# Convolution and feed-forward on one core: an inverse transform's buffer, two norms and two sums moved

## The chip, the cores and the metric

The kernel runs on one core of a Trainium2 chip. Its engines work side by side, each through its own list of instructions, and meet at semaphores: PE (TensorE, matrix products into PSUM), ACT (ScalarE), DVE (VectorE), POOL (GpSimd) and SP (SyncE, which here only issues transfers). PEld is PE's loading of weights. The metric is the device time of one execution in microseconds, lower is better. Before the change the median of three runs is 269.0 us (267.62 to 269.3).

## The reference

S = 2048 rows of D = 640 numbers, a feed-forward width of 1728, all in bfloat16. With `LN` a layer norm without weights, the core of it is:

```
k_shift[s] = sum over t < 4 of k[s - t] * shift_k[:, t]       # a causal convolution of 4 taps
kv         = k_shift * v
y          = causal convolution of kv with ssm_k over all 2048 rows (FFT) + kv * ssm_D
h          = q + LN(q) * y
out        = h + (silu(LN(h) @ w_gate) * (LN(h) @ w_up)) @ w_down
```

## The kernel before, in words

The 2048 rows are taken in four blocks of 512, named 0 to 3. The long convolution is done by blocks: every block of kv and every block of ssm_k is transformed by matrix products with cosine and sine tables (a transform of 256 odd frequencies, two planes for the real and the imaginary part), the products of block j of kv with block i - j of ssm_k are summed for output block i, and one inverse transform by matrix products gives y of block i.

For a block i the steps, with the names used in this document and their lines, are:

- `kv` (line 697): k's block is loaded transposed into the tile `kT` by a transposing transfer (line 514, issued by SP), v's block into `vt`. PE does the four taps as three groups of products with diagonal matrices (L717 and L712, "convolutions"), ACT evicts them to `kT` (L502), and for blocks 1 to 3 five transposing transfers turn them into `kvo`; DVE multiplies into `vt` (L748).
- `xfwd` (line 750): PE transforms `vt` in eight tasks of four products ("halves", L610) or, for block 2, eight tasks of two ("quarters", L647). ACT evicts each (L502); DVE combines them (L581, L656).
- `prod` (line 768): per pair of blocks and per half `f2`, DVE multiplies a transformed block by a kernel block twice (L779, L780, 2560 numbers a partition), adds and subtracts (L785, 1280 numbers), and for j > 0 adds the result to `Y` (L796, 2560 numbers). Last come the butterflies into `IE` and `IO` (L581), the inverse's input: sums and differences.
- `inverse` (line 847): PE makes four tiles of 128 rows (tasks 0 to 3; L860). Tasks 1 and 3 read `IO`, 0 and 2 read `IE`. Then, per tile, h and its layer norm (the "second norm"). In blocks 1 to 3 ACT evicts y to SBUF with a bias (L884), DVE multiplies it into `xh` (L887), ACT sums the row (L898) and sums its squares (L900). In block 0 (`ST`) one DVE instruction reads PSUM, multiplies and sums (L874), POOL makes the mean (L878), and ACT sums squares (L880). In both forms ACT adds epsilon (L904), POOL takes the power -1/2 (L911), and ACT (blocks 1 to 3: mean times scale L914, then L916) or DVE (block 0, L919) writes the normed row to `qo`. SP transposes it into `hnT` (L514).
- `ffn` (line 926, called ff0 to ff3): 14 "gate tasks" of PE (L941 and L942, ten products each; L952 for the narrow last), ACT's silu and copy (L964, L966), DVE's product (L968), then the "down tasks" (L1003) with two small pair tasks (L1015). In blocks 0 to 2 ACT evicts the result (L1023) and DVE adds it (L1030); SP writes the block out.

PSUM has four tiles of two banks (`units=4`), handed out by the planner in order of release. A task of PE that opens a tile waits for all who read the tile's earlier content.

What sets the order. Every instruction group is a numbered task with a cost estimate. `ORDER` is a written list of task numbers for each of the five engines; each engine issues strictly in it. `schedule` walks the lists with the estimated costs only to hand out PSUM tiles, to choose pauses and to place fill products; `emit` writes the waits. So an instruction of SP that waits (a transfer whose target is still being read) holds every later transfer of SP, and the same is true for POOL. Fill products (L250, 192 columns) are matmuls without use, which the planner puts where it expects PE to idle.

Memory is laid out by hand (lines 410 to 467). `kT` and `IO` share bytes, and so do `hnT` and `IE`. Because of that the load of block i + 1 of k cannot begin before the inverse of block i has read `IO`. `vt` has its bytes for itself. `VECTOR` lists the PSUM evictions that DVE does in place of ACT.

Of the kernel before, what the change touches and what calls it, by code (L numbers as in the profile page):

```python
# [11 lines left out]
ACTF = mybir.ActivationFunctionType  # L12
# [46 lines left out]
class _Graph:  # L59
# [87 lines left out]
    def schedule(self, order):  # L147
# [4 lines left out]
        for t in self.tasks:  # L152
            for d in t.deps | t.after:
                d.succ.append(t)
        seq = {e: [self.tasks[int(x)] for x in order[e].split()] for e in ENGINES}
        assert sorted(t.seq for e in ENGINES for t in seq[e]) == list(range(len(self.tasks)))
# [12 lines left out]
        while len(self.glob) < len(self.tasks):  # L169
# [22 lines left out]
            if t.opens is not None:  # L192
                pt = t.opens
                u = min((u for u in range(self.units) if unit_by[u] is None), key=lambda u: unit_free[u])
                pt.unit = u
                left[pt] = len(pt.users)
                t.late = t.deps - set(last_users.get(u, ()))
                t.deps.update(last_users.get(u, ()))
                if self.warm is not None and e == "pe" and at[e] > 2:
                    idle = s - max(free[e], unit_free[u])  # L200
                    t.fill = int((idle - 250) / 83) if idle > 700 else 0
                unit_by[u] = pt
# [28 lines left out]
    def emit(self, block):  # L231
# [77 lines left out]
    "pe": """  # L309
# [7 lines left out]
    """,  # L317
    "act": """
# [12 lines left out]
    """,  # L331
    "dve": """
# [10 lines left out]
    """,  # L343
    "pool": """
        8 10 6 11 5 9 7 151 202 216 195 205 209 219 198 212 134 336 135 403 421 394 412 529 610 619 628 601 736 822 813 840
        831
    """,
    "sp": """
# [3 lines left out]
    """,  # L352
}

VECTOR = """
    21 129
"""

def bass_sequential_preLN__ssm_conv_h3__swiglu_ffn__prompt_kernel(
# [38 lines left out]
    with ExitStack() as es:  # L398
# [23 lines left out]
        kT = sb("kT", o + 5120, [NC5, N + 16])  # L422
        IO = sb("IO", o + 5120, [2, 2, D])
        hnT = sb("hnT", o + 10400, [NC5, N])
# [43 lines left out]

        BN, DIRECT, D8, PT, BN2, ST, R4, PAIR, WARM, ACC, EA, KD, RD, LA, RA = (0,), (), (), (0,), (), (0,), ('xf2',), True, 24, (), True, (2, 3), (), (1, 2, 3), (0, 1, 2)
        g = _Graph(nc, es)  # L470
# [4 lines left out]
        def cact(n, ptr=0):  # L475
            return 60 + 0.833 * n + 93 * ptr

# [327 lines left out]
        def ln1(i):  # L805
# [18 lines left out]
            if EA:  # L824
                g.add("act", nm, lambda e: e.activation(out=s[:, 2, :], in_=s[:, 1, :], func=ACTF.Identity, bias=epc[:, 0:1]), 160,  # L825
                      r=[s[:, 1, :], epc[:, 0:1]], w=[s[:, 2, :]])
            else:
                g.add("pool", nm, lambda e: e.tensor_scalar(out=s[:, 2, :], in0=s[:, 1, :], scalar1=LN_EPS * D, scalar2=None, op0=ALU.add), 260,
                      r=[s[:, 1, :]], w=[s[:, 2, :]])
# [17 lines left out]
        def inverse(i):  # L847
# [18 lines left out]
            for j in range(4):  # L866
# [35 lines left out]
                if EA:  # L902
                    ep = epc[:, int(st):int(st) + 1]
                    g.add("act", nm, lambda e, m=m, ep=ep: e.activation(out=m[:, 2:3], in_=m[:, 1:2], func=ACTF.Identity, bias=ep), 160,  # L904
                          r=[m[:, 1:2], ep], w=[m[:, 2:3]])
# [7 lines left out]
                if i in LA:  # L913
                    g.add("act", nm, lambda e, m=m: e.activation(out=m[:, 4:5], in_=m[:, 0:1], func=ACTF.Identity, scale=m[:, 3:4]), 160,  # L914
                          r=[m[:, 0:1], m[:, 3:4]], w=[m[:, 4:5]])
# [10 lines left out]
        def ffn(i):  # L926
# [3 lines left out]
            for fb in range(14):  # L930
# [30 lines left out]
                for rows, ps_g, ps_u, ts in parts:  # L961
                    n = ts.stop - ts.start
                    uv, gv = u[rows, ts], gt[rows, 0:n]
                    g.add("act", nm, lambda e, pt=pt, gv=gv, a=ps_g, ts=ts: e.activation(out=gv, in_=pt.f(a[0], N, a[1])[:, ts], func=ACTF.Silu, scale=gain),  # L964
                          cact(n), w=[gv], pr=[pt])
                    g.add("act", nm, lambda e, pt=pt, uv=uv, a=ps_u, ts=ts: e.activation(out=uv, in_=pt.f(a[0], N, a[1])[:, ts], func=ACTF.Copy, scale=gain),  # L966
                          cact(n), w=[uv], pr=[pt])
                    g.add("dve", nm, lambda e, uv=uv, gv=gv: e.tensor_tensor(out=gv, in0=gv, in1=uv, op=ALU.mult),  # L968
                          cdve(n), r=[gv, uv], w=[gv])
            dn, pair = {}, ()  # L970
# [145 lines left out]
```

## Time and profile before

| what | us |
|---|---|
| median of three runs | 269.0 |
| the profiled execution | 268.22 |
| its span, first to last instruction | 266.3 |
| PE, DVE, ACT, POOL busy | 254.0, 204.0, 203.9, 29.1 |
| first gate task of ff0, ff1, ff2, ff3 begins | 52.5, 112.2, 170.0, 219.2 |
| last product of PE ends | 263.6 |

The profile is of one execution. A row of a group gives line, engine, operation, tiles, form and count, then the busy time in us, the mean of one in ns, and the idle time of the engine just ahead of it with what ended most of it. The chain of waits goes back from the last instruction to whatever released each step. A matmul's end is modelled, so consecutive matmuls overlap in the rows, and the same is true of ACT and DVE by about 0.1 us.

### The profile page before, as it was taken

The page shows a single profiled execution, that of the slowest core. Times are in us where ns is not written, and L with a number is a line of the kernel's source. Part 1 is how long each engine was busy: PE and PEld are TensorE (multiplying, and loading weights), DVE is VectorE, ACT ScalarE, POOL GpSimd, SP SyncE. Part 2 cuts the span into 40 slices and gives each one's busy share as a digit, 9 for nine tenths or more (in the row PEclk, how much of TensorE's full clock was granted, in tenths as well). Part 3 has the DMA queues.
Part 4 walks back from the last instruction along what each step waited for, and adds up shares of the span by engine and source line. Part 5 has one row for each costly group of instructions (what it writes and reads, how often), then busy time and mean ns, then how long its engine had stood idle before and what let it go on. Part 6 is the DMA issues. An engine that isn't in the chain of part 4 may idle for free.

```text
span 266.3 us, 4177 instructions
## 1 busy us (share of the span) xinstructions
PE 254.0 (95%) x1638; PEld 142.1 (53%) x1638; DVE 204.0 (77%) x285; ACT 203.9 (77%) x392; POOL 29.1 (11%) x37
## 2 busy tenths in 40 slices
PE   7889888999999999999999999899999999999995
PEld 5567454545544646544445567444446674444563
DVE  0889999999999999999999999999895101330404
ACT  2689999999967999766979999678799982653600
POOL 0000314202030035000020041000300200000000
PEclk9999999999999999999999999999999999999999
DMA  6998919889966566331001734510000140000032
GB/s 155 335 333 266 342 57 227 131 194 315 178 111 108 81 173 105 55 117 81 4 0 19 184 79 93 146 78 1 2 0 0 22 79 0 0 2 0 0 127 74
DMA packets 43701, 28.47 MB, mean 107 GB/s; under 512 B 32289, under 2 KB 41378, under 8 KB 43682
## 3 DMA queue, kind: packets, MB, share of 16 engines
q1 hardware_dynamic: 41968, 25.58, 36.4%
q0 software_dynamic: 1056, 2.62, 5.7%
q8 instruction: 13, 0.21, 0.3%
q10 hardware_dynamic: 658, 0.01, 0.1%
q14 instruction: 6, 0.05, 0.1%
HBM read 15.69 MB, written 2.62 MB: 69 GB/s over the span
## 4 chain that ended last, share of the span: by engine, by line
PE 53%; ACT 23%; DVE 11%; DMA 6%; SPq 4%; issue 2%; POOL 0%; DVEq 0%
PE ps L941 16%; PE ps L942 15%; PE ps L1003 14%; SPq L514 3%; ACT xh L843 3%; ACT KT L502 3%; PE ps L610 2%; DMA kT<-in_A_k_dram 2%; ACT KO L502 2%; DMA ftab<-cst_ftab 2%; DMA hnT<-qo 2%; DVE gu L968 2%; PE ps L717 2%; ACT C L502 1%; ACT qo L884 1%
## 5 line engine op out<-in xcount | busy, mean ns | idle before, releaser
L1003 PE MATMUL ps<-Wd,gu 128*128 128x384 bf16 (+1 forms) x390 | 55.5, 299 | 0.1
L941 PE MATMUL ps<-hnT,GA 128*128 128x512 bf16 x140 | 53.1, 379 | 1.3 <-DMA hnT<-qo 1.1
L942 PE MATMUL ps<-hnT,UA 128*128 128x512 bf16 x140 | 53.1, 379 | 0.0
L1003 PEld LDWEIGHTS ps<-Wd,gu 128*128 128x128 bf16 x390 | 37.6, 98 | 17.1 <-issue 1.1
L941 PE MATMUL ps<-hnT,GB 128*128 128x512 bf16 x120 | 45.5, 379 | 0.0
L942 PE MATMUL ps<-hnT,UB 128*128 128x512 bf16 x120 | 45.5, 379 | 0.0
L966 ACT ACTIVATE ub<-ps 128x512 bf16<-128x512 f32 (+1 forms) x60 | 33.9, 567 | 14.9 <-PE ps L942 12.0
L964 ACT ACTIVATE gu<-ps 128x512 bf16<-128x512 f32 x52 | 30.4, 596 | 13.2 <-PE ps L942 13.1
L968 DVE TENSOR_TENSOR gu<-gu,ub 128x512 bf16<-128x512 bf16 x52 | 21.5, 421 | 23.8 <-ACT gu L964 15.8
L779 DVE TENSOR_TENSOR T<-X,C 128x2560 bf16<-128x2560 bf16 x20 | 29.7, 1486 | 0.2
L780 DVE TENSOR_TENSOR T<-X,C 128x2560 bf16<-128x2560 bf16 x20 | 29.7, 1486 | 0.1
L911 POOL TENSOR_TENSOR mv<-mv,half 128x1 f32<-128x1 f32 x16 | 16.1, 1010 | 69.1 <-ACT mv L904 69.1
L941 PEld LDWEIGHTS ps<-hnT,GA 128*128 128x128 bf16 x140 | 13.7, 98 | 18.4 <-DMA hnT<-qo 1.4
L610 PE MATMUL ps<-KT,ftab 128*128 128x320 bf16 x128 | 19.8, 300 | 3.5 <-ACT KT L502 1.1
L942 PEld LDWEIGHTS ps<-hnT,UA 128*128 128x128 bf16 x140 | 13.7, 98 | 15.6
L785 DVE TENSOR_TENSOR T<-T 128x1280 bf16<-128x1280 bf16 x24 | 19.5, 820 | 0.2
L941 PEld LDWEIGHTS ps<-hnT,GB 128*128 128x128 bf16 x120 | 11.7, 98 | 14.2 <-ACT gu L964 0.2
L942 PEld LDWEIGHTS ps<-hnT,UB 128*128 128x128 bf16 x120 | 11.8, 98 | 14.0
L831 POOL TENSOR_TENSOR st<-st,half 128x8 f32<-128x8 f32 x4 | 8.3, 2067 | 88.1 <-ACT st L825 88.1
L796 DVE TENSOR_TENSOR Y<-Y,T 128x2560 bf16<-128x2560 bf16 x12 | 17.8, 1484 | 0.0
L610 PEld LDWEIGHTS ps<-KT,ftab 128*128 128x128 bf16 x128 | 11.2, 98 | 10.9 <-ACT KT L502 2.0
L843 ACT ACTIVATE xh<-xh,st 128x640 bf16<-128x640 bf16 x16 | 14.7, 967 | 2.7 <-DVE st L833 2.7
(96 smaller groups left out, 381.9 us busy)
## 6 DMA issues: line engine op xcount, KB each, us to landing
kc<-in_A_ssm_k_dram SPq DMA_DIRECT2D x4, 640.0 KB, 9.4
xh<-in_A_q_dram SPq DMA_DIRECT2D x4, 640.0 KB, 4.1
vt<-in_A_v_dram SPq DMA_DIRECT2D x4, 640.0 KB, 4.5
out_dram<-xh SPq DMA_DIRECT2D x15, 160.0 KB, 1.9
Wd<-in_B_w_down_dram SPq DMA_DIRECT2D x1, 1280.0 KB, 6.3
C<-C POOLq DMA_DIRECT2D x1, 1280.0 KB, 9.6
C<-R POOLq DMA_DIRECT2D x1, 1280.0 KB, 9.4
UA<-in_B_w_up_dram SPq DMA_DIRECT2D x1, 1120.0 KB, 9.1
```

Source lines behind the costliest of these rows:

```text
L610: last = e.matmul(pt.f(c, W), ftab[:, cs, j, f * P:(f + 1) * P], src[:, j, c * W:(c + 1) * W], start=(j == par), stop=(j == par + 2))
L779: g.add("dve", nm, lambda e, x=x, k=k, t1=t1: e.tensor_tensor(out=t1, in0=x, in1=k, op=ALU.mult), cdve(2560), r=[x, k], w=[t1])
L780: g.add("dve", nm, lambda e, x=x, k=ksw, t2=t2: e.tensor_tensor(out=t2, in0=x, in1=k, op=ALU.mult), cdve(2560), r=[x, k], w=[t2])
L785: g.add("dve", nm, lambda e, p=p, q=q, d=d, op=op: e.tensor_tensor(out=d, in0=p, in1=q, op=op), cdve(1280), r=[p, q], w=[d])
L796: g.add("dve", nm, lambda e, y=y, z=z: e.tensor_tensor(out=y, in0=y, in1=z, op=ALU.add), cdve(2560), r=[y, z], w=[y])
L843: g.add("act", nm, lambda e, j=j, xj=xj: e.activation(out=xj, in_=xj, func=ACTF.Identity, scale=s[:, 4, j:j + 1], bias=s[:, 5, j:j + 1]), ...
L941: e.matmul(pt.f(0, N), wg[:, c, f0:f0 + P], hnT[:, c, :], start=(c == 0), stop=(c == NC5 - 1))
L942: last = e.matmul(pt.f(1, N), wu[:, c, f0:f0 + P], hnT[:, c, :], start=(c == 0), stop=(c == NC5 - 1))
L964: g.add("act", nm, lambda e, pt=pt, gv=gv, a=ps_g, ts=ts: e.activation(out=gv, in_=pt.f(a[0], N, a[1])[:, ts], func=ACTF.Silu, scale=gain) ...
L966: g.add("act", nm, lambda e, pt=pt, uv=uv, a=ps_u, ts=ts: e.activation(out=uv, in_=pt.f(a[0], N, a[1])[:, ts], func=ACTF.Copy, scale=gain) ...
L968: g.add("dve", nm, lambda e, uv=uv, gv=gv: e.tensor_tensor(out=gv, in0=gv, in1=uv, op=ALU.mult), cdve(n), r=[gv, uv], w=[gv])
L1003: last = e.matmul(pt.flat(c1 - c0, P + c0), slots[fb][:, j * P:(j + 1) * P], Wd[:, fb, c0:c1], start=(fb == 0 and not second), stop=(fb == ...
```

## The change

Three edits of the computation, and a new order for all engines.

1. `IO` moves from the bytes of `kT` to those of `vt` (one line). k's next block now waits only for the transposes of this block's convolutions; v's next block waits for the inverse.
2. `ST` grows from block 0 to blocks 0, 1 and 2: the second norms of blocks 1 and 2 take the form with the DVE instruction from PSUM (L874, L878, L880) in place of the eviction, the product and the sum (L884, L887, L898). The apply stays on ACT. Block 2's first norm gets one small negation on DVE.
3. `ACC` grows from none to the pairs (1, 3) and (2, 3): their results go to the tile `ZB` (in the place of the kernel's block 3 transform) and are added to `Y` by four transfers that POOL issues with an adding operation, 640 KB each, in place of four DVE additions (L796).

With these the orders of all engines are replaced, the evictions that DVE takes (`VECTOR`) are two others, the fill products are named by task (`FILL`: six ahead of block 0's first convolution, eight ahead of block 1's) in place of being placed by the planner (eight and six in the trace), and some of the planner's cost estimates change.

What moves in the new order, of what the prediction speaks of: SP issues k's block 1 directly after GA and ahead of kc3, itab and UA; k's block 2 behind block 1's transposes and half of the weights; k's block 3 after the first of the four transposes of block 1's second norm. PE does the convolutions of block 2 within ff0's gate tasks and around the inverse of block 1, and those of block 3 within the start and the gate tasks of ff1, ahead of the inverse of block 2. The inverse of block 2 stands after the first down task of ff1. On ACT the mean-times-scale of a row of blocks 1 and 2 stands directly or nearly so after the epsilon of the same row.

```
-        IO = sb("IO", o + 5120, [2, 2, D])
+        IO = sb("IO", o, [2, 2, D])
...
-        ..., (0,), ('xf2',), True, 24, (), True, (2, 3), (), (1, 2, 3), (0, 1, 2)
+        ..., (0, 1, 2), ('xf2',), True, 24, ((1, 3), (2, 3)), True, (2, 3), (), (1, 2, 3), (0, 1, 2)
...
+        fills = dict(tuple(map(int, x.split(":"))) for x in FILL.split())
...
-                if self.warm is not None and e == "pe" and at[e] > 2:
-                    idle = s - max(free[e], unit_free[u])
-                    t.fill = int((idle - 250) / 83) if idle > 700 else 0
+                if self.warm is not None and e == "pe":
+                    t.fill = fills.get(t.seq, 0)
...
+FILL = "20:6 313:8"
...
 VECTOR = """
-    21 129
+    83 85
 """
```

`VECTOR` before: block 0's first convolution (1024 columns) and one half of kernel block 3. After: two halves of kernel block 1. The lists of `ORDER` are too long to print; the text above says what of them matters.

More of the change, by code (lines that the diff above doesn't have):

```diff
@@ L309 @@
     "pe": """
[7 rows of a table removed]
[7 rows of a table added]
     """,
     "act": """
[12 rows of a table removed]
[11 rows of a table added]
     """,
     "dve": """
[10 rows of a table removed]
[10 rows of a table added]
     """,
     "pool": """
-        8 10 6 11 5 9 7 151 202 216 195 205 209 219 198 212 134 336 135 403 421 394 412 529 610 619 628 601 736 822 813 840
-        831
+        10 5 6 8 9 11 7 151 202 216 209 205 219 195 212 198 134 336 135 414 417 398 406 409 390 401 393 525 618 621 610 602
+        594 613 605 597 767 772 777 782 729 815 806 833 824
     """,
     "sp": """
[3 rows of a table removed]
[3 rows of a table added]
     """,
 }
+FILL = "20:6 313:8"
 VECTOR = """
-    21 129
+    83 85
 """
@@ L467, in bass_sequential_preLN__ssm_conv_h3__swiglu_ffn__prompt_kernel @@
         assert o + 576 <= SBB + 16481 - A0, o + 576
-        BN, DIRECT, D8, PT, BN2, ST, R4, PAIR, WARM, ACC, EA, KD, RD, LA, RA = (0,), (), (), (0,), (), (0,), ('xf2',), True, 24, (), True, (2, 3), (), (1, 2, 3), (0, 1, 2)
+        BN, DIRECT, D8, PT, BN2, ST, R4, PAIR, WARM, ACC, EA, KD, RD, LA, RA = (0,), (), (), (0,), (), (0, 1, 2), ('xf2',), True, 24, ((1, 3), (2, 3)), True, (2, 3), (), (1, 2, 3), (0, 1, 2)
         g = _Graph(nc, es)
@@ L475, in cact @@
         def cact(n, ptr=0):
-            return 60 + 0.833 * n + 93 * ptr
+            return 60 + 0.833 * n + (93 * ptr if ptr < 2 else 219)
         def cdve(n):
@@ L824, in ln1 @@
             if EA:
-                g.add("act", nm, lambda e: e.activation(out=s[:, 2, :], in_=s[:, 1, :], func=ACTF.Identity, bias=epc[:, 0:1]), 160,
+                g.add("act", nm, lambda e: e.activation(out=s[:, 2, :], in_=s[:, 1, :], func=ACTF.Identity, bias=epc[:, 0:1]), 185,
                       r=[s[:, 1, :], epc[:, 0:1]], w=[s[:, 2, :]])
@@ L903, in inverse @@
                     ep = epc[:, int(st):int(st) + 1]
-                    g.add("act", nm, lambda e, m=m, ep=ep: e.activation(out=m[:, 2:3], in_=m[:, 1:2], func=ACTF.Identity, bias=ep), 160,
+                    g.add("act", nm, lambda e, m=m, ep=ep: e.activation(out=m[:, 2:3], in_=m[:, 1:2], func=ACTF.Identity, bias=ep), 185,
                           r=[m[:, 1:2], ep], w=[m[:, 2:3]])
@@ L913, in inverse @@
                 if i in LA:
-                    g.add("act", nm, lambda e, m=m: e.activation(out=m[:, 4:5], in_=m[:, 0:1], func=ACTF.Identity, scale=m[:, 3:4]), 160,
+                    g.add("act", nm, lambda e, m=m: e.activation(out=m[:, 4:5], in_=m[:, 0:1], func=ACTF.Identity, scale=m[:, 3:4]), 185,
                           r=[m[:, 0:1], m[:, 3:4]], w=[m[:, 4:5]])
@@ L964, in ffn @@
                     g.add("act", nm, lambda e, pt=pt, gv=gv, a=ps_g, ts=ts: e.activation(out=gv, in_=pt.f(a[0], N, a[1])[:, ts], func=ACTF.Silu, scale=gain),
-                          cact(n), w=[gv], pr=[pt])
+                          max(400, cact(n)), w=[gv], pr=[pt])
                     g.add("act", nm, lambda e, pt=pt, uv=uv, a=ps_u, ts=ts: e.activation(out=uv, in_=pt.f(a[0], N, a[1])[:, ts], func=ACTF.Copy, scale=gain),
-                          cact(n), w=[uv], pr=[pt])
+                          max(400, cact(n)), w=[uv], pr=[pt])
                     g.add("dve", nm, lambda e, uv=uv, gv=gv: e.tensor_tensor(out=gv, in0=gv, in1=uv, op=ALU.mult),
-                          cdve(n), r=[gv, uv], w=[gv])
+                          max(320, cdve(n)), r=[gv, uv], w=[gv])
             dn, pair = {}, ()
```

63 rows, old and new, of the table ORDER are left out of this document.

## The prediction

> **What bounds the kernel now.** I read the page's busy shares first, then busy time by stretch, then the chain of waits and the timeline at the places where PE stands still, and the groups by form for prices.
>
> ```profile
> PE 254.0 (95%) x1638; PEld 142.1 (53%) x1638; DVE 204.0 (77%) x285; ACT 203.9 (77%) x392; POOL 29.1 (11%) x37
> ```
>
> The columns of the next view are the stretch, its length, and the busy time of PE, PEld, DVE, ACT and POOL, then clock and DMA share.
>
> ```profile
> 0.00:17.30 17.30, 14.16 (x130) 9.81 (x131) 8.61 (x15) 8.60 (x11) 0.63 (x11) 1.00 0.92 261
> 17.30:52.50 35.20, 31.52 (x274) 20.39 (x273) 34.48 (x51) 34.99 (x58) 6.95 (x9) 1.00 0.77 214
> 52.50:88.00 35.50, 35.50 (x182) 17.38 (x181) 35.09 (x49) 30.18 (x58) 4.57 (x3) 1.00 0.78 178
> 88.00:112.00 24.00, 23.02 (x181) 14.00 (x178) 23.75 (x29) 22.23 (x47) 5.92 (x4) 1.00 0.61 115
> 112.00:142.00 30.00, 29.83 (x141) 13.70 (x142) 29.52 (x41) 23.19 (x50) 1.89 (x1) 1.00 0.14 45
> 142.00:171.00 29.00, 27.80 (x218) 17.76 (x216) 28.78 (x36) 28.18 (x55) 4.36 (x4) 1.00 0.49 115
> 171.00:266.30 95.30, 92.22 (x523) 49.09 (x521) 43.75 (x69) 56.49 (x117) 4.81 (x5) 1.00 0.11 28
> ```
>
> There are two regimes. From 17.3 to 52.5 ACT is busy 34.99 of 35.20 us (it empties PSUM) and PE only 31.52: this stage ends when ACT does. From 52.5 on PE is the bound: idle 0.00, then 0.98 (88 to 112), 0.17, 1.20 (142 to 171), and 3.08 in the last stretch, most of it the tail after the last product. DVE looks full up to 171 (35.09 of 35.50), but it fills its time with products of later blocks, and PE does not wait for it. So the matmul work, which the change leaves as it is, sets the end; only PE's waits can be won. The waits at the two block boundaries:
>
> ```profile
> 88.69 2.35 PE L860 MATMUL ps<-IE,itab 128*128 128x320 bf16 x16
> 94.37 1.06 PE L717 MATMUL ps<-kT,dg 64*64 64x512 bf16 x16 [0.61 <-DMA kT<-in_A_k_dram]
> 148.12 1.25 PE L860 MATMUL ps<-IE,itab 128*128 128x320 bf16 x8
> 170.05 0.39 PE L941 MATMUL ps<-hnT,GA 128*128 128x512 bf16 x1 [1.09 <-DMA hnT<-qo]
> ```
> ```profile
> 88.61 3.61 SPq L514 DMA_TRANSPOSE kT<-in_A_k_dram  x1
> 103.01 6.39 SPq L514 DMA_TRANSPOSE hnT<-qo  x4
> ```
> ```profile
> SPq L514 <- PE ps L860: 55.2, 2, 28.2
> ```
> ```profile
> PE ps L860 <- ACT qo L884: 0.4, 1, 0.4
> ```
> ```profile
> 25.19 2.26 ACT KT L502 x2
> 29.34 0.60 ACT KO L502
> 47.81 2.17 PE ps L610 x16
> 98.69 7.06 PE ps L1003 x52
> 105.75 0.38 PE ps L1015 x4
> 110.87 1.25 ACT FO L502 x2
> 112.17 0.39 PE ps L941
> 149.31 0.72 ACT qo L898 x2
> 150.03 0.68 ACT qo L884
> 153.24 0.91 ACT kT L502
> 165.69 4.31 DMA hnT<-qo
> ```
>
> The load of k's next block stands in SP's queue until the inverse has read IO (55.2 us in two waits), starts at 88.61, and costs PE 0.61 at 94.37. At 112.17 PE waits for evictions (ACT FO), at 170.05 for the transposed second norm (1.09), and in the last stretch 0.4 at the inverse of block 3 (L860).
>
> **The change part by part.** Prices by form:
>
> ```profile
> L796 DVE TENSOR_TENSOR Y<-Y,T 128x2560 bf16<-128x2560 bf16 x12 | 17.8, 1484 | 0.0
> L779 DVE TENSOR_TENSOR T<-X,C 128x2560 bf16<-128x2560 bf16 x20 | 29.7, 1486 | 0.2
> L785 DVE TENSOR_TENSOR T<-T 128x1280 bf16<-128x1280 bf16 x24 | 19.5, 820 | 0.2
> L874 DVE SCALAR_TENSOR_TENSOR xh<-ps,st,xh 128x640 bf16<-128x640 f32 x4 | 3.4, 882 | 0.0
> L874 DVE DVE_READ_ACCUMULATOR xh<-ps,st,xh 128x1 f32 x4 | 0.3, 84 | 0.0
> L887 DVE TENSOR_TENSOR xh<-xh,qo 128x640 bf16<-128x640 bf16 x12 | 5.7, 487 | 6.5 <-ACT qo L884 6.5
> L610 PE MATMUL ps<-KT,ftab 128*128 128x320 bf16 x128 | 19.8, 300 | 3.5 <-ACT KT L502 1.1 <-DVE vt L736 0.8 <-ACT R L502 0.7
> ```
> ```profile
> C<-C POOLq DMA_DIRECT2D x1, 1280.0 KB, 9.6
> UA<-in_B_w_up_dram SPq DMA_DIRECT2D x1, 1120.0 KB, 9.1
> hnT<-qo SPq DMA_TRANSPOSE x16, 2.8
> kT<-in_A_k_dram SPq DMA_TRANSPOSE x4, 5.7
> q0 software_dynamic: 1056, 2.62, 5.7%
> ```
> ```profile
> L911 POOL TENSOR_TENSOR mv<-mv,half x16: 547/900/2164, 42.6 to 214.3; 128x1 f32<-128x1 f32 x16
> ```
>
> *IO in v's place.* k's blocks 1 to 3 now wait only for the transposes of the block before; v's wait for the inverse instead. k2 is loaded behind block 1's transposes, near 55 us, and first used in the middle of ff0's gate products: the 0.61 at 94.37 goes. v2 lands some 4 to 5 us after its inverse products, and xf2 follows in the new order only after about three down products of 3.53 (7.06 / 2): covered. If that cover went, each us would be PE's. On SP, k1 stands ahead of kc3, itab and UA in the load phase; k2 and k3 ahead of block transposes. k3's issue (3.61 by k2's row) stands ahead of three of block 1's four hnT transposes; they do not become ready before it is out, so I count 0, with 3.61 as the other end.
>
> *Second norms of blocks 1 and 2 from PSUM.* For each of 8 rows of tiles ACT loses an eviction and a sum, 0.68 + 0.72 = 1.40 us start to start: 5.6 us a block. DVE exchanges 487 for 882 + 84 ns: +0.48 x 8 = +3.8 us. POOL gets 8 small means, of the order of the 900 ns of its powers at most. What it does to the path is the time from the last inverse product to the last hnT transpose. Block 2: that product ends near 149.3, the norm is there at 170.0, 20.7 us, in which ACT has no rest. Off come 5.6, and kv3's three evictions (0.91 + 0.91 + about half of that = 2.3), which the new order does before the inverse: 12.8 us. PE's cover in the new order: four groups of pair and down products, 3 x 3.53 + 2 x 0.38, and six forward tasks of 0.54 (2.17 / 4) = 14.6 us. Margin 1.8, so the 1.20 of that stretch goes. Block 1: from 91.0 to the last hnT, whose transpose is issued in the last quarter of the 6.39 us from 103.01 and lands 2.8 later, 110.9: 19.9 us. Off 5.6 and 2.3; two more evictions stand ahead of the last row (0.60 + 0.68): 13.3. Cover: 3 x 3.53 + 0.38, seven quarter tasks of 0.27 (half of 0.54) and k3's third convolution (a little under 1): 13.8. Margin 0.5, so I leave 0.3 of the 0.98.
>
> The weak place is ACT's queue: each row's mean-times-scale now stands straight behind POOL's power (547 to 2164 ns), with the next rows behind it. With 900 ns it is inside the sums above; at 2164 it would add 1.3 a block and eat the margins. [...]
>
> *Two product sums by transfers.* Four DVE additions of 1.484 go (-5.9 us), four transfers of 640 KB come, issued by POOL. The nearest row takes 9.6 us for 1280 KB: 4.8 if it scales, 9.6 if not. In the new order DVE writes the same buffer again after three products, four half operations and four additions of 640: 3 x 1.486 + 4 x 0.820 + 4 x 0.487 = 9.7 us of other work, a little less start to start. Even the long end costs DVE under 1 of the 5.9 us won, and PE sees 0, since iv3's tasks keep their place behind ff2's gates. If this cover went, DVE would stand in front of the fourth buffer write and iv3 would be late us for us. POOL's queue holds the power of ln3 behind the four issues; DVE uses it two products and three shorter operations after it wrote the last sum, over 4 us later. With DVE lighter, the 0.4 at iv3 should go; I count 0.3.
>
> *Evictions, order, fills.* One eviction of 1024 columns and one of 640 go from DVE to ACT, two of 640 come back. In the ACT-bound stage ACT is two evictions of 0.60 lighter and one heavier, -0.6; the one of 1024 lies in its early idle time. Eight fill products before k1's first convolution (192 columns, some 0.08 each against 2.17 / 16 for 320) stand on PE near 42 us, where it is nearly full: +0.6. I count 0, ends -0.6 and +1.2. The other constants only move the planner's estimates.
>
> *Sum.* Won: 0.98 - 0.3 (k's 0.61 is in it), 1.20 and 0.3: 2.2 us. The profiled execution, 268.22 us with a span of 266.3, would take 266.0; it lies 0.8 below the median of the runs shown, 269.0 (267.62 to 269.3). From the median: 266.8 us.
>
> **The rivals.** *All waits go.* Every wait from 52.5 on: 0.98 + 0.17 + 1.20 + 0.4 = 2.75. A matmul's end is modelled: L610 shows 300 ns for one where 16 take 2.17 us, 0.136 each, so idle time shows each wait some 0.16 short; with eight waits 4.0 us, 265.0 us. For it: the margins above. Against: block 1's is 0.5.
>
> *The transposes meet the transfer.* The first transfer of block 3 is issued about when block 2's hnT transposes are. Two transfers of 1280 KB took 5.7% of 266.3 = 15.2 us of all 16 engines, so one of 640 KB takes 3.8. hnT then comes up to 3.8 late, the margin of 1.8 turns into a wait of 2.0 and the gain into nothing: 269.0 us. The 4.31 us of the transpose at 165.69, against a median of 2.8, shows that it can be held up. [...]
>
> *k's early load is late (slower).* k1's transposes come in the phase with DMA share 0.92 and 0.77, directly behind GA. The new order wants them for kv1's third convolution, which stands behind xf0's evictions (to 25.19 in the trace) and two of KT (2.26): about 27.5 us; PE takes its tasks in order, so ACT would soon stand too. Issued at some 18 us, when the convolution of k0 is done with the buffer, and landing 5.7 later (median), they cost nothing. Behind a load like UA, 9.1 us, they land at 18 + 9.1 + 5.7 = 32.8 and cost 5.3 us of the ACT-bound stage, one for one: 272.1 us. It costs from a landing at 27.5 on, and is a loss on the whole from 29.7.
>
> **How the numbers follow.** Forecast 266.8 (266.1 to 268.2): 0.35. All waits go, 265.0 (264.3 to 266): 0.25. Transposes meet the transfer, 269.0 (to 270.3): 0.15. k late, 272.1 (270 to 274): 0.25. The measurement tells about 1% (2.7 us) from no change: faster is under 266.3, slower over 271.7. Faster: 0.25 and 0.05 of the forecast, 0.30. Slower: 0.18 of the last case. Same: 0.52. The range that leaves out about 1 in 10 on each side is 264.3 to 272.5.
>
> **What would show it.** No wait of PE for k between 88 and 95; ff2's first gate product about 3 us earlier than 170 less the two forward products that now follow it, without a wait for hnT; no DVE wait at the fourth to tenth operation after the first transfer; ff0's first gate product within 1 us of 52.5. Wrong would be: that product later than 54 (the load of k, or ACT waiting early), ACT waiting for POOL in blocks 1 and 2, or DVE standing before iv3.

## The result and the profile after

The changed kernel takes 266.59 us in the median of 9 runs (265.74 to 267.31), the kernel before 269.0 us beside it (9 runs, 267.62 to 269.54). The ratio is 0.9917, with a 95% interval of 0.9892 to 0.9941. The profiled execution took 266.08 us with a span of 264.1; its counterpart before took 268.22 with 266.3. The span is 2.2 us shorter. Medians in this document leave out one run, 276.97 us of the kernel with k late, which lies over 1.5% above the fastest run of its kernel.

The first view is the page's line of busy times, the second the busy time by stretch, with the columns of the prediction (stretch, length, PE, PEld, DVE, ACT, POOL, granted clock, DMA share, GB/s).

```profile
PE 253.2 (96%) x1621; PEld 141.9 (54%) x1638; DVE 200.8 (76%) x290; ACT 194.7 (74%) x368; POOL 38.8 (15%) x49
```
```profile
17.30:52.50 35.20, 31.64 (x268) 19.58 (x269) 34.18 (x50) 34.21 (x57) 6.81 (x9) 1.00 0.95 246
52.50:88.00 35.50, 35.34 (x198) 16.91 (x200) 35.17 (x49) 29.02 (x58) 5.66 (x3) 1.00 0.83 166
88.00:112.00 24.00, 23.89 (x170) 15.78 (x170) 23.37 (x33) 20.33 (x39) 7.42 (x8) 1.00 0.63 127
112.00:142.00 30.00, 29.75 (x160) 13.26 (x162) 29.76 (x41) 23.20 (x48) 2.01 (x1) 1.00 0.08 27
142.00:171.00 29.00, 28.95 (x200) 18.74 (x200) 28.73 (x42) 21.63 (x42) 9.03 (x10) 1.00 0.52 114
171.00:266.00 95.00, 88.52 (x499) 47.22 (x502) 40.96 (x66) 56.21 (x116) 7.24 (x7) 1.00 0.23 49
```

From 88 to 112 PE now stands 0.11 us in place of 0.98, from 142 to 171 it stands 0.05 in place of 1.20. ACT is 6.55 us lighter in the second of these (21.63 for 28.18). The gates come early, as PE's timeline shows: the first gate or up product that it has of ff0, ff1 and ff2.

```profile
52.12 0.38 PE L943 MATMUL ps<-hnT,UA 128*128 128x512 bf16 x1
...
110.66 0.38 PE L942 MATMUL ps<-hnT,GA 128*128 128x512 bf16 x1
...
165.17 0.38 PE L943 MATMUL ps<-hnT,UA 128*128 128x512 bf16 x1
```

ff2 starts at 165.17 and not at 170.05. Two halves of xf3, which the order before had done by then, are still to come (1.08 us), so PE is 3.8 us ahead. At the end it is 2.2 ahead: 1.6 us are given back in block 3. PE's timeline shows where: four waits, 0.42 + 0.37 + 0.66 + 0.25 = 1.70 us, where the kernel before had one, of 0.35 at the same inverse.

```profile
186.05 1.25 PE L953 MATMUL ps<-hnT,PK 128*128 128x512 bf16 x4 [0.42 <-ACT ub L967]
...
189.83 0.39 PE L942 MATMUL ps<-hnT,GB 128*128 128x512 bf16 x1 [0.37 <-ACT ub L967]
...
197.15 2.35 PE L861 MATMUL ps<-IO,itab 128*128 128x320 bf16 x16 [0.66 <-DVE IO L582]
199.74 0.45 PE L861 MATMUL ps<-IE,itab 128*128 128x320 bf16 x2 [0.25 <-DVE IE L582]
```

The timelines of DVE and POOL lead to a cause. The small product of ln3 (L834) stands in DVE's queue ahead of block 3's last products and of ff2's gate products. It waits for the power on POOL, which takes 2.70 us and starts only when ACT has the sums of x3, and ACT got x3 late:

```profile
186.20 0.42 DVE L969 TENSOR_TENSOR gu<-gu,ub 128x512 bf16<-128x512 bf16 x1
187.91 0.16 DVE L834 TENSOR_TENSOR st<-st 128x4 f32<-128x4 f32 x1 [1.29 <-POOL st L832]
```
```profile
185.11 2.70 POOL L832 TENSOR_TENSOR st<-st,half 128x8 f32<-128x8 f32 x1 [1.72 <-ACT st L826]
```
```profile
174.99 0.74 ACT L819 ACTIVATE qo<-xh 128x640 bf16<-128x640 bf16 x1 [2.09 <-DMA xh<-in_A_q_dram]
```

x3 goes into the buffer that block 1's output writes leave, so its load waits for them. In the kernel before it was issued at 171.38, here at 170.04, though PE is 3.8 us ahead. The chain of waits that ended last runs through these pieces (start, length, what; cut), from the last write over x3 and the power to the inverse of block 3:

```profile
166.51 3.51 DMA out_dram<-xh
170.04 4.93 DMA xh<-in_A_q_dram
...
185.11 2.71 POOL st L832
...
199.74 1.26 PE ps L861 x8
```

Two theories for block 3 went into the experiments. Theory 1: DVE's work and its order ahead of iv3 hold PE up, and the transfers are what makes room. Theory 2: the transfers hold up the output writes and x3, and cost what they save. Then each part was tried alone and undone.

### The profile page after: what moved, and what is told of

It is laid out like the page before. It is cut to its first block, busy times and chain, and to the rows that moved or that the text cites. A ratio compares the mean times of both kernels' runs of the same rounds, so it can differ in the third digit from the quotient of the medians.

```text
span 264.1 us, 4164 instructions
## 1 busy us (share of the span) xinstructions
PE 253.2 (96%) x1621; PEld 141.9 (54%) x1638; DVE 200.8 (76%) x290; ACT 194.7 (74%) x368; POOL 38.8 (15%) x49
## 4 chain that ended last, share of the span: by engine, by line
PE 65%; DVE 13%; ACT 7%; DMA 6%; SPq 4%; issue 2%; POOL 1%; DVEq 0%
PE ps L943 16%; PE ps L1004 16%; PE ps L942 15%; PE ps L611 6%; PE ps L861 5%; SPq L515 3%; DVE T L781 3%; DVE T L780 2%; DMA ftab<-cst_ftab 2%; PE ps L718 2%; DMA xh<-in_A_q_dram 2%; DVE Y L786 1%; PE ps L986 1%; DMA out_dram<-xh 1%; ACT qo L822 1%
## 5 line engine op out<-in xcount | busy, mean ns | idle before, releaser
L942 PE MATMUL ps<-hnT,GA 128*128 128x512 bf16 x131 | 49.7, 379 | 0.0
L942 PE MATMUL ps<-hnT,GB 128*128 128x512 bf16 x118 | 44.8, 379 | 0.4 <-ACT ub L967 0.4
L912 POOL TENSOR_TENSOR mv<-mv,half 128x1 f32<-128x1 f32 x16 | 14.6, 915 | 34.1 <-ACT mv L905 34.1
L832 POOL TENSOR_TENSOR st<-st,half 128x8 f32<-128x8 f32 x4 | 9.6, 2400 | 64.2 <-ACT st L826 64.2
L611 PE MATMUL ps<-vt,ftab 128*128 128x320 bf16 x96 | 14.5, 299 | 0.0
L503 ACT ACTIVATE KT<-ps 128x1280 bf16<-128x1280 bf16 x8 | 10.3, 1362 | 3.7 <-PE ps L569 3.7
```

The lines of the kernel that those rows point to most:

```text
L611: last = e.matmul(pt.f(c, W), ftab[:, cs, j, f * P:(f + 1) * P], src[:, j, c * W:(c + 1) * W], start=(j == par), stop=(j == par + 2))
L912: g.add("pool", nm, lambda e, m=m: e.tensor_tensor(out=m[:, 3:4], in0=m[:, 2:3], in1=half[:, 1, 0:1], op=ALU.pow), 650, r=[m[:, 2:3], half ...
L942: e.matmul(pt.f(0, N), wg[:, c, f0:f0 + P], hnT[:, c, :], start=(c == 0), stop=(c == NC5 - 1))
```

## The experiments

Each was timed beside the kernel before on the same chip; that one's median was 268.56 to 269.06 us. Ratios are to it. The changed kernel was not timed again in these rounds, and the kernel before was up to 0.4 us faster in them than beside it; a difference of two medians here carries that, so small ones are given by the ratios as well. In the diffs a line of numbers is a queue of ORDER, cut to the places that change.

| kernel | us | ratio, 95% interval |
|---|---|---|
| changed kernel | 266.59 | 0.9917 (0.9892 to 0.9941) |
| without transfers | 269.39 | 1.004 (1.0023 to 1.0056) |
| transfers for p23 only | 267.13 | 0.9956 (0.9932 to 0.998) |
| transfers alone, on the kernel before | 275.45 | 1.0275 (1.0244 to 1.0305) |
| small product of ln3 later | 265.43 | 0.9898 (0.9869 to 0.9926) |
| additions earlier | 265.11 | 0.989 (0.9848 to 0.9933) |
| both | 264.44 | 0.9844 (0.9817 to 0.987) |
| norms alone, on the kernel before | 277.32 | 1.0314 (1.0278 to 1.0349) |
| norms undone | 276.7 | 1.029 (1.026 to 1.0321) |
| input's place alone, on the kernel before | 268.88 | 1.0 (0.998 to 1.0019) |
| convolutions of k2 behind the inverse | 281.31 | 1.0458 (1.043 to 1.0486) |
| k late | 274.49 | 1.0214 (1.0171 to 1.0256) |
| fewer fills | 267.0 | 0.9937 (0.9917 to 0.9958) |

### Without the transfers

```diff
-    pool  ... 597 767 772 777 782 729 ...
+    pool  ... 597 729 ...
-    dve   ... 766 484 ... 771 760 ... 776 762 ... 781 785 ...
+    dve   ... 766 767 484 ... 771 772 760 ... 776 777 762 ... 781 782 785 ...
-    ACC = ((1, 3), (2, 3))
+    ACC = ()
```

> The changed kernel with its four product sums of block 3 put back on DVE, each straight behind the operation that writes its operand; nothing else moves. DVE gets 4 x 1.48 = 5.9 us more before iv3. Theory 1 (DVE's work ahead of iv3 is what PE waits for in block 3 of the changed kernel, and the transfers take 5.9 us of it away): DVE swallows the 1.29 us that it stands before ln3's power and the 0.6 of other idle time there, and the remaining 4 us come out as a longer PE wait before iv3, 270 to 271 us. Theory 2 (DVE has room there, and the transfers only hold up the output writes and x3's load): no new wait before iv3, x3 lands about 1 us earlier than its 174.97, 266 to 267 us.

Measured: 269.39 us, 2.8 more than the changed kernel (3.3 by the ratios). Theory 1 has the sign and most of its 3.4 to 4.4 us: the transfers are worth some 3 us, for 5.9 us of DVE's work. Theory 2's mechanism is there as well, only smaller: the list of DMA issues between 150 and 195 us (operation, count, KB each, median us to landing), first of the changed kernel, then without transfers, then of the transfers alone on the kernel before.

```profile
Y<-ZB POOLq DMA_DIRECT2D x4, 640.0 KB, 5.8
out_dram<-xh SPq DMA_DIRECT2D x4, 160.0 KB, 3.7
xh<-in_A_q_dram SPq DMA_DIRECT2D x1, 640.0 KB, 4.9
...
hnT<-qo SPq DMA_TRANSPOSE x4, 2.6
```
```profile
out_dram<-xh SPq DMA_DIRECT2D x4, 160.0 KB, 1.9
xh<-in_A_q_dram SPq DMA_DIRECT2D x1, 640.0 KB, 3.7
...
```
```profile
Y<-ZB POOLq DMA_DIRECT2D x4, 640.0 KB, 7.0
out_dram<-xh SPq DMA_DIRECT2D x4, 160.0 KB, 5.1
xh<-in_A_q_dram SPq DMA_DIRECT2D x1, 640.0 KB, 4.8
...
hnT<-qo SPq DMA_TRANSPOSE x4, 5.7
```

With transfers a write takes 3.7 us and not 1.9, x3 takes 4.9 and not 3.7: the writes and the load get through beside the transfers, which take 5.8 us each in the median, and take longer themselves.

### The transfers alone

```diff
-    dve   ... 726 774 488 ... 492 779 501 ... 785 784 787 ... 767 789 643 ...
+    dve   ... 726 488 ... 492 501 ... 785 787 ... 767 643 ...
-    pool  ... 601 736 ...
+    pool  ... 601 774 779 784 789 736 ...
-    ACC = ()
+    ACC = ((1, 3), (2, 3))
```

> The kernel before with the four product sums as transfers issued by POOL, at the same places of the order; all else, the order of the other instructions too, as before. By theory 1 DVE is 5.9 us lighter but ff2's gates are tied by the order to block 2's inverse and second norm as before, so only the 0.4 to 0.5 us that PE waits at iv3 and what DVE held up of ff2 can go: 268.0 to 268.7 us against 269.0. By theory 2 the output writes and x3's load come 1 us or more later and ff2 is held up: 269.5 to 271 us.

Measured: 275.45 us, 6.9 slower than the kernel before, past both theories. The third fence above tells why: the block's transposes took 5.7 us in the median. In the order before POOL still has the powers of block 2 ahead, so the first two transfers go out together at 163.64, straight into the last two hnT transposes (issued 165.00 and 167.04), which landed at 173.81 and 175.78. PE's timeline (fill products that the plan put there, then the gate):

```profile
169.60 6.85 PE L250 MATMUL ps<-ident 128*128 128x192 bf16 x81
176.50 0.38 PE L942 MATMUL ps<-hnT,UA 128*128 128x512 bf16 x1
```

The output writes and x3 follow late (x3 lands at 185.40), and DVE waits 2.7 us for its buffer in two waits:

```profile
DVE ZB L785 <- DMA Y<-ZB: 2.7, 2, 1.6
```

This is the prediction's rival of the transposes that meet the transfer. It is real, and dearer than the 2.0 us worked out for it; the changed order avoids it, since there the last hnT transpose is issued at 160.44 and the first transfer at 161.18.

### The transfers of p23 only

```diff
-    ACC = ((1, 3), (2, 3))
+    ACC = ((2, 3),)
-    pool  ... 597 767 772 777 782 729 ...
+    pool  ... 597 777 782 729 ...
-    dve   ... 766 484 ... 771 760 ...
+    dve   ... 766 767 484 ... 771 772 760 ...
```

> The changed kernel with the sums of p13 put back on DVE, those of p23 left to transfers. If it is the first two transfers that hold up block 1's output writes and x3's load, the writes take 2 us again and x3 lands at 173.0 to 173.8 as without any transfer, in place of 174.97; DVE gets 3.0 us more, of which its wait before ln3's power (1.29) takes part, and iv3 comes 1.2 to 1.7 us later: 267.8 to 268.3 us. If the writes are slow for another reason, x3 lands at 175 or later and the time goes to 268.5 to 269.6.

Measured: 267.13 us. The list of DMA issues has the writes and x3 as fast as without transfers, and x3 landed at 173.64:

```profile
out_dram<-xh SPq DMA_DIRECT2D x4, 160.0 KB, 1.9
xh<-in_A_q_dram SPq DMA_DIRECT2D x1, 640.0 KB, 3.8
```

So the first two transfers are what slows the writes. They win 0.5 us (267.13 to 266.59; 1.0 by the ratios) for 3.0 us of DVE's work, the last two, which go out after x3 has landed, 2.3 (269.39 to 267.13). The 0.5 lies at the edge of what these intervals tell apart.

### One instruction later, three additions earlier

The first edit moves ln3's small product (730) behind two instructions:

```diff
-    dve   ... 660 730 786 640 787 ...
+    dve   ... 660 786 640 730 787 ...
```

The second moves the last three residual additions of block 1 (488, 493, 497):

```diff
-    dve   ... 766 484 769 768 493 488 770 497 773 ...
+    dve   ... 766 484 488 493 769 497 768 770 773 ...
```

> The changed kernel with one DVE instruction moved: the small mean-times-scale product of ln3, which waits for POOL's power, goes from ahead of the fourth half operation of p33.0 to behind that and one gate product. If the 1.29 us that DVE stood there at 187 is what delays the gate product for ff2's seventh gate and iv3's halves, DVE runs through, and of PE's 0.53 + 0.83 + 0.41 us of gaps at 189.8, 197.2 and 199.7 about 1.0 goes: 265.3 to 265.8 us. If DVE is simply full there, or PE's gaps come from ACT's order, the wait goes from one place to the next and the time stays at 266.4 to 266.8.

Measured: 265.43 us, 1.16 less than the changed kernel (0.5 by the ratios). DVE runs through at the place in question, and of L861's two waits for IO (1.8 us in the changed kernel) only the early one at iv0 is left:

```profile
188.06 0.42 DVE L969 TENSOR_TENSOR gu<-gu,ub 128x512 bf16<-128x512 bf16 x1
188.51 0.16 DVE L834 TENSOR_TENSOR st<-st 128x4 f32<-128x4 f32 x1
```
```profile
PE ps L861 <- DVE IO L582: 1.1, 1, 1.1
```

The two intervals overlap over more than half of their lengths; with the next edit added they no longer do. The traces say it more closely: from the end of the products ahead of the narrow gate task (L953) to the first product of IE in iv3 PE takes 13.2 us (186.07 to 199.28) for 14.1 (185.63 to 199.74), 0.9 less. The edit takes no work away, so what it won, 0.5 to 1.2 us, was the place in DVE's queue and not the amount of its work.

> The changed kernel with block 1's last three residual additions on DVE put ahead of the products that stood between them, so that the output writes of block 1 are issued 2 us earlier; all else as in the changed kernel. If x3's load, which waits for these writes to leave its buffer, sets ln3 and through it DVE's wait of 1.29 us, x3 lands at 172.5 to 173.5 in place of 174.97, the wait at ln3's power falls under 0.3, and PE's gaps in block 3 shrink by about 1 us: 265.3 to 265.9. If the first transfer (issued at 161.2) holds the writes up, x3 still lands after 174 and the time stays at 266.4 to 266.8.

Measured: 265.11 us, but that is no run's time: three lie from 263.88 to 264.11 and three from 266.11 to 267.19. The profiled run is the slowest of them, and there both halves of the expectation met: the writes went out 3 us earlier and ran into the transfer the longer (5.4 us in the median), x3 landed at 176.09, and DVE stood 1.22 us. No trace of the faster three was kept.

> The changed kernel with both moves on DVE: the small product of ln3 later, block 1's residual additions earlier. If DVE standing before ln3's power is the whole of what the moves can win, they don't add: 265.0 to 265.6 us. If the earlier output writes free x3's load in runs in which the transfers let them through, the two add: 264.0 to 264.8 us.

Measured: 264.44 us (264.1 to 265.04), 2.2 less than the changed kernel and 4.5 less than the kernel before. Here the same writes took 5.3 us and x3 landed at 173.86. This version's runs lie within 0.9 us, the one above within 3.3, which would fit a late x3 that matters less once the small product is out of its way; no trace of this version with a late x3 shows it. In the traces of these versions the power of ln3 follows x3: x3 at 173.86, 174.97 and 176.09 (both moves, the changed kernel, additions earlier) goes with a power that starts at 184.09, 185.11 and 186.23. Why the same order of issues let x3 land at 176.09 in one execution and 173.86 in another stays open.

### The norms alone, and undone

On the kernel before, for the four rows of blocks 1 and 2 (names of tasks, since their numbers shift):

```diff
-    act   iv1 ev1 ... iv1 sum1 sq1 ...      dve  iv1 mul1 ...
+    act   iv1 sq1 ...                        dve  iv1 stt1 ...      pool  iv1 mean1 pow1 ...
-    ST = (0,)
+    ST = (0, 1, 2)
```

> The kernel before with the second norms of blocks 1 and 2 read from PSUM and nothing else of the change: ACT loses its eviction and its sum for each row of tiles (8 x 1.4 us), DVE's product of 487 ns becomes one of 966, POOL gets a small mean; every other instruction keeps its place. Theory 1 (DVE has no room before iv3, so the norms need the transfers): ff2's first gate comes about 1 us earlier, but DVE's 8 x 0.48 = 3.8 us more come out ahead of iv3, less the 0.6 us that DVE idles there now: 269.5 to 272 us against 268.6. Theory 2 (DVE has room in blocks 1 and 2, since it works ahead there): the whole wait for the transposed norm goes, 267.0 to 267.8 us.

Measured: 277.32 us, 8.4 slower, past both theories. What the trace shows is a matter of order more than of DVE's total. PE stands in the two block stretches (2.7 us of it for the products from PSUM, 2.5 for the product with v), ACT is idle for a third of it and more, and the clock goes under 1 (two stretches at half speed, which cost PE's products 3.4 us in this execution; the last section):

```profile
88.00:112.00 24.00, 20.12 (x155) 12.01 (x154) 21.36 (x29) 14.18 (x31) 8.23 (x8) 0.96 0.59 106
142.00:171.00 29.00, 25.24 (x175) 14.43 (x174) 27.07 (x40) 18.75 (x36) 7.37 (x7) 0.94 0.31 69
```

The four products from PSUM lie between products of the next block on DVE, and the small mean waits on POOL behind a power of another row; ACT's square in turn waits for that mean:

```profile
98.29 2.94 POOL L910 TENSOR_TENSOR mv<-mv,half 128x1 f32<-128x1 f32 x1 [5.49 <-ACT mv L903]
```
```profile
101.76 0.83 ACT L879 ACTIVATE qo<-xh,mv 128x640 bf16<-128x640 bf16 x1 [2.63 <-POOL mv L877]
```

The opposite edit leaves the new order and takes the norms back (DVE's product of 487 ns, ACT's eviction and sum):

> The changed kernel with the second norms of blocks 1 and 2 done as before (ACT's eviction and sum, DVE's product of 487 ns in place of the 966 from PSUM, no small means), all else in the new order: the two first evictions stand ahead of the first row's sum, the other two ahead of the second's. By the prediction's chains (13.3 and 12.8 us against covers of 13.8 and 14.6) 5.6 us more in each block make waits of 5.1 before ff1's gates and 3.8 before ff2's, less what DVE's 3.8 us lighter load gives back ahead of iv3: 272.5 to 275.5 us. Rival: the order alone made the gain and ACT has idle time that takes most of the 5.6 us: 266.5 to 269 us.

Measured: 276.7 us, 10.1 more than the changed kernel and over the range; the chains of the prediction gave 8.9, and no relief on DVE shows. The wait for hnT is back, and the last of its transposes met the transfer: issued at 169.45, landed at 175.42. Here, too, two waits of PE bring a stretch at half clock each, 3.4 us of its products in this execution (276.85 us). Not all of that comes out in the time: one run with a mean clock of 1.000 took 275.52.

```profile
PE ps L944 <- DMA hnT<-qo: 2.9, 1, 2.9
```

### The input's place alone, and the convolutions put back

```diff
-        IO = sb("IO", o + 5120, [2, 2, D])
+        IO = sb("IO", o, [2, 2, D])
```

> The kernel before with half of the inverse's input at v's place and nothing else of the change. k's load for block 2 no longer waits for the inverse's products and its 0.6 to 0.8 us at the convolution (94.4) go. Theory 1: nothing is late next, 267.8 to 268.1 us against 268.6. Theory 2: PE comes to ff1's first gate 0.6 us earlier, but the evictions ahead of it on ACT end when they did (112.2), and the wait only moves there: 268.4 to 268.8. The load of v may also be late, as it now waits for the inverse: 269 to 270.

Measured: 268.88 us against 268.91: nothing. k2 now landed at 72.42 and PE's wait for it is gone, but the last of the convolutions' transposes takes 4.4 us to land for 2.4 before, so the last product with v begins when it did (104.90 for 104.52), and PE waits for the products with v instead:

```profile
PE ps L647 <- DVE vt L748: 1.1, 1, 1.1
```

In the changed kernel (the other way round isn't to be had, as the new order needs k early) the three convolutions of k2 went back behind the inverse:

```diff
-    pe    ... 502 ... 506 386 510 388 291 387 292 293 385 297 ...
+    pe    ... 386 388 387 385 291 502 292 506 293 510 297 ...
-    act   503, 507 and 511 ahead of the inverse's rows       sp  500 504 229 ...
+    act   ... 288 503 ... 399 507 ... 418 511 ...            sp  500 229 504 ...
```

> The changed kernel with the three convolutions of k's block 2, and their evictions, put back behind block 1's inverse, as the order before had them; k itself still lands early (62.4 us). It shows what the early landing is worth beside the 0.61 us of waiting for k. Theory: the early load pays by letting the convolutions, their evictions and the transposes behind them run ahead of the inverse; put back, their evictions (0.91 + 0.91 + 0.45 = 2.3 us by the prediction's rows) stand in block 1's chain, and the product with v, done at 97.9 in the changed kernel, comes some 5 us later, behind which xf2's first quarter waits: PE stands 3 to 5 us before xf2 or ff1's first gate, 269.5 to 272.5 us. Rival: the convolutions bring PE as much cover as their evictions take, the 0.61 us is all that the early load is worth, and the time stays within 1 us: 266.3 to 267.6.

Measured: 281.31 us, 14.7 more: the theory's sign at three times its size. DVE stands 11.75 us at the first product with v, everything behind it with it, and PE waits for that product. What that product waits for is v itself, and this comes from SP's list as the edit leaves it: v's load stands there behind three transposes of the convolutions, which now wait, so it was issued at 103.34 in place of 91.28. So the 14.7 us price the late convolutions and the late v together (and 1.9 us of products at half clock, from 110 to 115 us of the profiled execution); with v's load ahead of the transposes it wasn't tried.

```profile
107.79 0.43 DVE L749 TENSOR_TENSOR vt<-vt,kvo 128x512 bf16<-128x512 bf16 x1 [11.75 <-DMA vt<-in_A_v_dram]
```
```profile
PE ps L648 <- DVE vt L749: 4.9, 1, 4.9
```

### k late, and fewer fills

```diff
-    sp    ... 222 311 67 4 223 319 ...
+    sp    ... 222 67 4 223 311 319 ...
```

> The changed kernel with the load of k for block 1 put behind the loads of kc3, itab and UA in SP's queue, so that it lands late; in the changed kernel it lands at 24.28 and PE waits 0.3 us for it. Theory (the prediction's slower case): it lands at 29 to 33 us, PE and with it ACT stand from 24.5 on, and each microsecond past that comes out in the time one for one: 271 to 275 us. Rival: the stage has room for it, since ACT finds other evictions ready, and less than half of the lateness comes out: 267 to 269 us.

Measured: 274.49 us, 7.9 more. k landed at 30.80 for 24.28, 6.5 us later, so it cost more than one for one; products at half clock (the last section) can account for the excess.

```profile
PE ps L713 <- DMA kT<-in_A_k_dram: 6.3, 1, 6.3
```

```diff
-FILL = "20:6 313:8"
+FILL = "20:6"
```

> The changed kernel without the eight fill products of 192 columns before the first forward product of k3 (the six at the start stay). By the prediction's term they take 8 x 0.08 = 0.6 us of PE where it is nearly full near 42 us: ff0's first gate comes 0.6 us earlier and the time is 266.0 us. Rival: PE waits there for ACT's evictions anyway, and the gate comes when it did, within 0.2 us: 266.4 to 266.8.

Measured: 267.0 us, so nothing won. Without the fills PE waits longer for the eviction that it waited for anyway (0.9 us in the changed kernel):

```profile
PE ps L611 <- ACT kT L503: 1.5, 1, 1.5
```

## Why the prediction came out, point by point

The forecast was 266.8 us, and 266.0 for the profiled execution; 266.59 and 266.08 came. The sum is right, two of its terms are not, and they cancel: that it came out within 0.2 us is luck, though the mechanism of the norms' term is as forecast.

- *IO in v's place.* PE's wait for k went, as said. The step "the 0.61 at 94.37 goes" took the wait for its price, though: alone the edit is worth 0.0 us, because the product with v was late next. What the early load is worth is what the new order builds on it, the convolutions and what hangs on them ahead of the inverse, and with these put back 14.7 us go, of which the late v load of that edit has a part that the runs don't separate. The prediction had counted of this only ACT's 2.3 us. It had seen the danger, though: if v's cover went, it said, each us would be PE's, and with v late it did go.
- *The norms.* Right in mechanism and in size: both chains ended inside their cover, with no wait at 110.66 or 165.17. From the end of the last inverse product to the landing of the last hnT transpose it is 12.8 us in block 1 (97.0 to 109.8, for 13.3) and 12.7 in block 2 (150.3 to 163.0, for 12.8). ACT did wait for POOL (0.96 and 2.05 us for small means), which the prediction had listed as a sign of being wrong; the chains held all the same. The power's mean was 915 ns here, close to the 900 taken, and the longest of the 16 took 1782, under the 2164 that the prediction put at 1.3 us a block. With the norms alone one took 2.94 us, as shown above; what makes a power longer, no run shows.

```profile
L912 POOL TENSOR_TENSOR mv<-mv,half 128x1 f32<-128x1 f32 x16 | 14.6, 915 | 34.1 <-ACT mv L905 34.1
```

- *The size of the early gains.* 0.68 + 1.20 = 1.9 us were counted up to ff2; 3.8 came. Idle time shows each wait some 0.16 us short, as the first rival said; its sum without iv3, 0.98 + 0.17 + 1.20 and eight times 0.16, is 3.6. So that rival's sum comes near up to ff2's gate, where 0.4 us of the 3.8 are ff0's gate, which came early (52.12 for 52.5).
- *The transfers.* They took 5.6 to 8.7 us, 5.8 in the median, between the ends of 4.8 and 9.6, and DVE waited for the buffer only once, 0.20 us at 178. The step that failed is "POOL's queue holds the power of ln3 behind the four issues; DVE uses it [...] over 4 us later", and with it "the 0.4 at iv3 should go". The power didn't wait for the issues: POOL was free 1.72 us before it. It waited for ACT, ACT for x3, and x3 for writes that the transfers slowed; the prediction had followed POOL's queue and not what the power itself needs. In place of 0.3 us won, 1.6 were lost in block 3. The sign it had named, DVE standing before iv3, is in the trace. Of that loss 0.5 to 1.2 us is the small product's place, as its move shows. Without the first two transfers x3 lands at 173.64 and DVE doesn't stand there, but its 3.0 us more of work come out elsewhere.
- *The fills and evictions.* Counted at 0, with a term of +0.6 for the fills; 0 it is for the fills, as PE waited there in any case; the moved evictions weren't tried by themselves.
- *The rivals.* The transposes that meet a transfer, and the late k, did not come, but both are real: 8.7 us for a transpose under two transfers (167.04 to 175.78), and 7.9 us for a k that lands 6.5 us late.

No part pays in the order before: 0.0, +8.4 and +6.9 us alone there, and -2.4 together in the new order. Whether one of them alone would pay in an order of its own wasn't tried, and neither was the new order without any of them, which needs the early k.

## What to carry to other kernels

An engine that takes its work in a fixed order can be late by its head as well as by its load: before moving work off it, look for the small instruction that waits there for a chain through other engines, and move that first (here one instruction, 0.5 to 1.2 us). The same holds for a queue of transfers: a load behind a transfer that waits is late with it (v's with the convolutions put back, issued at 103.34 for 91.28). A part that gains only with a new order can't be priced in the old one, so its waits are worth what the order does with them; and a DMA put in place of engine work is to be priced by what is in flight beside it, both for it (5.6 to 8.7 us here) and for the others (a write of 3.7 us for 1.9).

## What was not expected of the hardware

In these runs a stand of PE could cost more than its length. With the norms undone PE stood for 2.07 of 3 us, and the granted clock (the column before the last two) then was half for 3.4 us. Waits of up to 1.1 us left it at 1.00 in the kernels before and after, and so did one of 1.86 us without transfers and one of 1.91 with transfers for p23 only. The rows are of the norms undone:

```profile
105.00:106.00 1.00, 0.00 (x1) 0.00 (x0) 0.97 (x3) 1.00 (x4) 0.69 (x1) 1.00 0.28 63
106.00:107.00 1.00, 0.32 (x2) 0.11 (x2) 1.00 (x1) 1.00 (x3) 0.19 (x1) 1.00 1.10 195
107.00:108.00 1.00, 0.61 (x6) 0.16 (x6) 1.00 (x2) 1.00 (x3) 0.00 (x0) 1.00 1.28 290
108.00:109.00 1.00, 1.00 (x6) 0.67 (x7) 0.71 (x1) 0.97 (x3) 0.00 (x0) 0.75 1.16 246
109.00:110.00 1.00, 1.00 (x6) 0.55 (x4) 0.00 (x0) 1.00 (x5) 0.00 (x0) 0.50 0.42 80
110.00:111.00 1.00, 1.00 (x6) 0.54 (x5) 0.00 (x0) 1.00 (x2) 0.55 (x1) 0.50 0.00 0
111.00:112.00 1.00, 1.00 (x6) 0.60 (x5) 0.53 (x2) 0.97 (x3) 0.00 (x0) 0.55 0.02 4
```

(0.25 + 0.5 + 0.5 + 0.45 us lost is 1.7 us.) Each of the two kernels with the norms alone and undone has two such stretches, 3.4 us. By these waits the edge seems to lie near 2 us, which is an estimate: with transfers for p23 only, nine of twelve runs took 266.82 to 267.46 us at a mean clock of 0.999 to 1.0, and three took 268.55 to 269.13 at 0.994, which is 1.6 us of 265. That would be one such stretch, but no trace of these three was kept. The same is in the kernel with k late, where PE waited 6.3 us; some 5 us of its products after that ran at half clock, which costs 2.5 us. There PE stood from 25 us on and the clock was still 1.00 up to 29, so the estimate doesn't say when within a stand it goes down:

```profile
31.00:34.00 3.00, 2.75 (x9) 1.33 (x9) 3.00 (x4) 0.00 (x0) 0.00 (x0) 0.50 0.03 5
34.00:36.00 2.00, 2.00 (x10) 0.99 (x8) 0.66 (x1) 1.09 (x2) 0.00 (x0) 0.50 0.00 0
```
